# A new opening for a planned kernel of linear attention and a gated MLP: load order, fillers, first chunk, and the cost figures of the planner

## The chip, the core and the metric

The kernel runs on one core of one Trainium2 chip. A core has a matrix engine (PE, with its weight loads PEld), a vector engine (DVE), an activation engine (ACT), GpSimd (POOL) and SyncE (SP), which here only issues DMAs. The metric is the device time of one execution in microseconds (us). All inputs lie in HBM when the clock starts, the output has to be there when it stops.

## The reference, cut to what matters

For each of 4 x 8 heads a 48 x 48 state is read by q, corrected by k and v, token by token over 768 tokens; the result of all heads is the input of a gated MLP with 1536 hidden features.

```python
k_n = k / (norm(k) + 1e-6)
for t in range(S):
    y[:, :, t] = einsum('bhd,bhde->bhe', q[:, :, t], state)
    v_old = einsum('bhde,bhd->bhe', state, kt)
    state = state + bt * einsum('bhd,bhe->bhde', kt, vt - v_old)
x = y.transpose(0, 2, 1, 3).reshape(B * S, H * D)
out = (x @ w_a) * (x @ w_b) @ w_out
```

## The kernel before, in words

The 768 tokens are cut into 24 chunks of 32. Inside a chunk the recurrence is a triangular system, so a chunk needs: `prep` (norms of k, Gram matrices G of k and q on PE, scaled by `dc` on DVE), `solve` (a serial run of some 30 small DVE operations for four chunks at once, then transposes), and `steps`, a chain of small matmul groups per chunk with a copy by ACT or DVE between any two: W and X (they finish the solve of the first four chunks, behind an `eye` matmul), K (state times k, not for chunk 0), U (the corrected values), A (the output y), S (the state's update). Each group is 32 small matmuls, four of them side by side on four 32-row strips of PE, and since f32 goes through PE in two passes, it shows as 64 records. U, K and A write the two banks of the tile `duo`, S writes `S_ps`. Two chunks of y, transposed, are one tile `xb` of the MLP: per block of 128 hidden features (12 blocks) six matmuls `bank<-xb,wt`, a copy by ACT, a product by DVE, and two matmuls `bank<-wt,g` back. The first two pairs of chunks (24 MLP units) run in f32, the other ten in f16 halves after `split` has made these.

The weights come as 64-bit words, 1.15 MB a block, into three slots (`late` and two in `stage`); three DVE operations (`decode`) make f32 weights of a block in `wt` and free the slot. `scales` squares each block on ACT and sums the squares on PE (`bank<-one,sqw`).

Nothing is issued where it is written. Every call is noted as an `Op`, and `Plan.pack` lists them: a model of each engine's time, of the banks, of the DMAs (`MOVE`), of the matrix engine's clock and of its instruction blocks (`BLOCK`, `EDGE`, `FETCH`, `stall`) chooses for each engine which op comes next, by priorities that start from due times (`when`, `slot`). The planned order is then the program order of each engine. Until `UNTIL` one bank is kept aside, and where the model has PE at rest it puts fillers into that bank: matmuls `bank<-ones` of 128x512, whose result nobody reads (`issue`, line 484; all other instructions have line 493). `load` adds a DMA to SP's list; SP issues in order, and a load into a slot waits until the decode before it has read the slot. `hold` holds the number of the op that ends group A of chunk 1.

Of the kernel before, what the change touches and what calls it, by code (L numbers as in the profile page):

```python
# [26 lines left out]
P = 128  # L27
# [10 lines left out]
BASE, FRESH, UNIT = 46e3, 4.6e3, 3.75e3  # L38
# [11 lines left out]
def slot(c, piece):  # L50
    if c < 2:
        v = {
            0: {"W": -10, "X": -9, "U": -8, "S": -7, "A": -3.9},
            1: {"W": -6.9, "K": -6, "X": -5.9, "U": -5, "A": -4, "S": 0.2},
        }[c].get(piece, -30)
    elif c < 4:
        v = (c - 2) * 5 + {"W": 0.7, "X": 1.2, "K": 1.5, "U": 2.5, "S": 3.5, "A": 4.5}.get(piece, -30)
    elif piece == "G":
        v = 0.3 + 5 * (c // 2 - 2) if c < 8 else finish(c // 4 * 4 - 4 + c % 4 // 2) - 0.5
# [19 lines left out]
class Plan:  # L79
# [129 lines left out]
    def add(self, eng, fn, name, args, kw):  # L209
# [14 lines left out]
        if eng == "SP":  # L224
            op.dur = 475.0
            n = mybir.dt.size(outs[0].dtype)
            for d in outs[0].shape:
                n *= d
            op.move = max(n / 250.0, 20.0)
# [63 lines left out]

    def pack(self, pri, back=False):
# [10 lines left out]
        pos, edge, come, small = 0, self.EDGE, 0.0, False  # L305
        kept = 0 if back else 1
        vacant, held, blocked = [(k, {}) for k in range(len(self.pool) - kept)], {}, []
        fill = {}
# [3 lines left out]
        while len(done) < n:  # L312
# [56 lines left out]
            if not back and not o.banks and self.HOLD:  # L369

                soon = t + min(self.HOLD, 0.8 * o.dur)
                nxt_ = [r for r, k in wait[e] if t < r < soon and pri[k] < pri[i] - self.MARGIN]
                if nxt_:
                    heapq.heappush(can[e], (pri[i], i))
                    for x in can[e]:
                        heapq.heappush(wait[e], (min(nxt_), x[1]))
                    can[e] = []
                    continue
            at[i] = t
            if e == "PE" and not back:  # L380

                if kept:
                    f, took, many = max(free[e], self.SINCE), self.IDLE * (1 if warm else 2), 0
                    while f + took <= t:
# [3 lines left out]
                        took = self.IDLE * (1 if warm else 2)  # L388
                        use, f, many = use + took, f + took, many + 1
                    fill[i] = many  # L390
                    for _ in range(many):
                        pos += 4
                        if pos > edge:
                            edge, come = edge + self.BLOCK, t + self.FETCH
# [24 lines left out]
            if e == "SP":  # L419
                if back:  # L420
                    end = t + o.dur + self.MOVE[0] + o.move + self.MOVE[1]
                else:
                    dma = max(dma, t + o.dur + self.MOVE[0]) + o.move
                    end = dma + self.MOVE[1]
            done.append(i)
# [11 lines left out]
    HOLD = 300.0  # L437
# [4 lines left out]
    def order(self):  # L442
# [23 lines left out]
        for i, o in enumerate(ops):  # L466
            if o.banks and o.eng != "PE":
# [12 lines left out]
    def issue(self, tc):  # L480
        with tc.manual_schedule():
            for i in self.order():
                for _ in range(self.fill.get(i, 0)):
                    self.nc.tensor.matmul(  # L484
                        self.pool[-1][:, 0:512],
                        self.idle,
                        self.idle.unsqueeze(1).broadcast_to([P, 4, P]),
# [9 lines left out]
def tile_kernel(ctx, tc, kqt, kn, vn, beta, w, masks, picks, out):  # L497
# [88 lines left out]
    plan.idle = ones  # L586
    sqf = one("sqf", [P, 768])
# [29 lines left out]
    def decode(b):  # L617
        load(b, "w")
        st, d = slots[b % 3].rearrange("p (a l) -> p l a", l=2), wt[:, plain(b) : plain(b) + WD]
        lo, hi = st[:, 0], st[:, 1]  # L620
        V.tensor_scalar(d, hi, 5, 2, op0=ALU.logical_shift_left, op1=ALU.logical_shift_right)
# [3 lines left out]
        yield  # L625

# [96 lines left out]
    def load(c, what):  # L723
        if (c, what) in loaded:
            return
        loaded.add((c, what))
        if what == "w":
            SP.dma_start(slots[c % 3], w[c].bitcast(I32))
        elif what == "b":
            SP.dma_start(bt, beta)  # L730
            SP.dma_start(mk, masks)
        elif what == "m":
# [8 lines left out]
    def prep(g):  # L741
# [61 lines left out]
    def solve(g):  # L803
# [29 lines left out]
        V.transpose(XT.rearrange("p t u -> p (t u)"), X.rearrange("p t s -> p (t s)"))  # L833
        if HALVES[g]:

            xn = xnt.rearrange("p (a b) -> p a b", b=32)
            V.transpose(xn, X.rearrange("p t s -> p s t")[:, 0:16])
# [46 lines left out]
    def steps(g, chs):  # L884

        for c in chs:
            first, last = c == 0, c == NCH - 1
            rw, k2, vt = raw(c), knc(c), vnc(c)
            if HALVES[g]:
                join(g, c)  # L890
            if first:
                fs = [vt, vt]
            else:
                sh = shr()
                A.copy(sh, S_ps[0:KR, :, 0:384])
                plan.due = slot(c, "K")
                with plan.group():
# [14 lines left out]
            with plan.group():  # L912
                for q, h4, _, cols in heads():
                    T.matmul(
                        duo[tok(h4), h4 % 2, cols],
                        tts[c][tok(h4), q],
                        fs[h4 % 2][tok(h4), cols],
# [13 lines left out]
            with plan.group():  # L931
                for q, h4, a, cols in heads():
                    T.matmul(
                        duo[tok(h4 ^ 1), h4 % 2, cols],
                        ats[c][tok(h4), q],
                        u[tok(h4), h4 % 2, cols],
# [6 lines left out]
            if not last:  # L943
                plan.due = slot(c, "S")
                with plan.group():
                    for q, h4, a, cols in heads():
# [3 lines left out]
                            u[tok(h4), h4 % 2, cols],  # L950
# [6 lines left out]
            for h4 in range(4):  # L957
                A.copy(
                    y32[tok(h4 ^ 1)].rearrange("p (j b e) -> p b j e", j=3, b=4),
                    duo[tok(h4 ^ 1), h4 % 2, 0:384].rearrange("p (b j e) -> p b j e", b=4, j=3),  # L960
                )
            if c // 2 < FULL:
# [173 lines left out]
    for b in range(1, 3):  # L1136
        run_all(ws[b])
    run_all(st[0])
    queue.extend((s, list(range(NFC))) for s in range(2))
    load(0, "m")  # L1140
# [12 lines left out]
    def opening():  # L1153
        yield next(pr[1])
        for n in range(2):
            yield next(pr[1])
            yield next(pr[1])
            for _ in range(3):
                yield next(rest)
# [98 lines left out]
```

## Time and profile before

| | us |
|---|---|
| three runs | 636.98, 637.65, 635.96 (median 636.98) |
| profiled execution | 635.62, of which span 633.6 |
| PE busy | 614.3 |
| DVE busy | 411.1 |
| ACT busy | 305.0 |
| mean granted clock of PE | 0.978 |

The span runs from the first to the last instruction. Busy times are unions of an engine's instructions; PE also counts the fillers. The clock is given as a share of 2.4 GHz; PE runs at either 2.4 or 1.2 GHz (0.5).

### The profile page before, as it was taken

The numbers are of one execution on the slowest core, as the hardware profiler recorded it, in microseconds if no ns is written. First come the engines' busy times: TensorE is split into PE (matmuls) and PEld (weight loads), VectorE is DVE, ScalarE is ACT, GpSimd is POOL, SyncE is SP. The second block draws the span as 40 slices with busy tenths as digits, with TensorE's granted clock in tenths as the row PEclk, the third lists the DMA queues.
The fourth block names the chain that finished last, engine by engine and source line by source line (L and its number), as shares of the span: only waits on it lengthen the run. The fifth ranks groups of instructions, "written<-read, shape, count | busy, mean of one in ns | idle before, by whom it ended". The sixth has DMA issues, their size and how long they took to land.

```text
span 633.6 us, 25222 instructions
## 1 busy us (share of the span) xinstructions
PE 614.3 (97%) x11486; PEld 475.5 (75%) x11486; DVE 411.1 (65%) x1106; ACT 305.0 (48%) x750; POOL 23.8 (4%) x29
## 2 busy tenths in 40 slices
PE   8977989999999999999999999999999999999997
PEld 4445867777777878877878787887787787787785
DVE  4795597987779994389855589743788443244222
ACT  3043313458783475435654553654355455445322
POOL 0000030001000001100010000101000000000000
PEclk9966899999999999999999999999999999999999
DMA  9837456100200200301303103001000000000000
GB/s 278 286 137 254 172 178 206 40 25 3 85 27 28 85 27 28 110 2 37 103 3 111 28 3 110 27 4 53 2 4 27 3 27 3 3 26 2 26 1 26
DMA packets 10715, 41.19 MB, mean 65 GB/s; under 512 B 1200, under 2 KB 4656, under 8 KB 7728
## 3 DMA queue, kind: packets, MB, share of 16 engines
q1 hardware_dynamic: 10608, 39.57, 19.2%
q8 instruction: 90, 1.47, 1.0%
q14 instruction: 17, 0.14, 0.1%
HBM read 34.85 MB, written 4.72 MB: 62 GB/s over the span
## 4 chain that ended last, share of the span: by engine, by line
PE 86%; DVE 6%; ACT 6%; issue 2%; ACTq 0%
PE bank L493 67%; PE duo L493 13%; PE S_ps L493 3%; PE bank L484 3%; DVE b L493 2%; ACT wt L493 2%; ACT sqf L493 1%; DVE wt L493 1%; ACT y L493 1%; DVE tmp L493 1%; ACT sqy L493 0%; ACT a L493 0%; DVE at L493 0%; DVE g L493 0%; ACT tt L493 0%
## 5 line engine op out<-in xcount | busy, mean ns | idle before, releaser
L493 PE MATMUL bank<-xb,wt 128*128 128x256 f16 (+1 forms) x1800 | 247.8, 291 | 0.0
L493 PEld LDWEIGHTS <-wt 128*128 128x128 f16 x2160 | 208.3, 98 | 35.9 <-issue 1.0
L493 DVE TENSOR_TENSOR g<-bank,a 128x256 f32<-128x256 f32 x144 | 60.8, 423 | 128.3 <-ACT a L493 126.8
L493 PE MATMUL bank<-wt,ghl 128*128 128x384 f16 x720 | 136.5, 326 | 0.0
L493 ACT ACTIVATE a<-bank,gs 128x256 f32<-128x256 f32 x120 | 56.8, 474 | 147.7 <-PE bank L493 147.1
L493 PEld LDWEIGHTS <-ghl 128*128 128x128 f16 x720 | 67.2, 98 | 34.9
L493 PE MATMUL bank<-stage,wt 128*128 128x256 f16 x648 | 76.9, 273 | 0.0
L493 DVE TENSOR_TENSOR ghl<-g,ghl 128x256 f16<-128x256 f32 x120 | 52.0, 433 | 28.8 <-ACT ghl L493 27.9
L493 ACT CAST ghl<-g 128x256 f16<-128x256 f32 x120 | 48.3, 402 | 44.9 <-DVE g L493 44.3
L493 PEld LDWEIGHTS bank<-xb,wt 128*128 128x128 f32 x288 | 55.0, 194 | 12.8 <-issue 1.0
L493 DVE TENSOR_TENSOR b<-b,tmp 128x31 f32<-128x31 f32 (+20 forms) x170 | 56.6, 333 | 4.1
L493 DVE TENSOR_TENSOR tmp<-b,b 128x31 f32<-128x31 f32 (+20 forms) x170 | 56.3, 331 | 4.1
L493 ACT COPY y<-duo 32x384 f32<-32x384 f32 x96 | 45.1, 470 | 4.7 <-PE duo L493 3.6
L493 PE MATMUL bank<-wt,g 128*128 128x384 f32 x96 | 37.7, 511 | 0.0
L484 PE MATMUL bank<-ones 128*128 128x512 f32 x54 | 30.4, 713 | 3.0 <-DVE ones L493 3.0
L493 ACT COPY a<-bank 128x256 f32<-128x256 f32 x24 | 8.8, 369 | 41.6 <-PE bank L493 41.5
L493 PEld LDWEIGHTS duo<-sh,rawb 48*64 48x64 f32 x1216 | 20.2, 139 | 8.4 <-DVE at L493 3.5
L493 POOL TENSOR_TENSOR vnb<-vnb,nm 128x384 f32<-128x384 f32 x20 | 18.8, 963 | 176.5 <-DVE nm L493 83.2
L493 ACT COPY u<-duo 128x768 f32<-128x768 f32 (+1 forms) x27 | 20.2, 749 | 10.8 <-PE duo L493 7.0
L493 PE MATMUL duo<-sh,rawb 48*64 48x48 f32 x1216 | 22.6, 225 | 2.7 <-DVE at L493 1.8
L493 PEld LDWEIGHTS S_ps<-u,knb 32*48 32x48 f32 x1216 | 16.8, 126 | 10.9 <-issue 5.8
L493 DVE TENSOR_TENSOR f<-vnb,duo 128x768 f32<-128x768 f32 x23 | 21.8, 949 | 4.4 <-PE duo L493 4.0
(107 smaller groups left out, 586.5 us busy)
## 6 DMA issues: line engine op xcount, KB each, us to landing
stage<-in_w SPq DMA_DIRECT2D x8, 1152.0 KB, 7.2
rawb<-in_kqt SPq DMA_DIRECT2D x10, 896.0 KB, 5.9
vnb<-in_vn SPq DMA_DIRECT2D x12, 384.0 KB, 5.5
late<-in_w SPq DMA_DIRECT2D x4, 1152.0 KB, 6.5
out<-ob SPq DMA_DIRECT2D x24, 192.0 KB, 1.9
knb<-in_kn SPq DMA_DIRECT2D x10, 384.0 KB, 3.6
late<-in_kqt SPq DMA_DIRECT2D x2, 896.0 KB, 6.5
late<-in_kn SPq DMA_DIRECT2D x2, 384.0 KB, 4.3
```

What stands on the lines that cost most here:

```text
L484: self.nc.tensor.matmul(self.pool[-1][:, 0:512], self.idle, self.idle.unsqueeze(1).broadcast_to([P, 4, P]), start=True, stop=True, skip_gr ...
L493: fn(*(self.place(a, lease) for a in args), **{k: self.place(a, lease) for k, a in kw.items()})
```

## The change

The planner's figures change: `BASE` and `UNIT` of the due times are lower, loads over 1 MB are taken to be faster, an instruction block takes 2500 ns longer while DMAs run (`BUSY`), the waiting rule `HOLD` is replaced by one that holds until 40 us (`CALM`), and operations of ACT and DVE that read `duo` are given the priority of those that free a bank. Fillers may now be 128x128 (narrow) or 128x512, chosen by the length of the rest, and end at 42 us instead of 60; before everything else PE gets 47 small matmuls 32x48 on one 32x32 corner of the array (`PADS`).

Loads: beta comes second, the masks ahead of the first v, and four weight blocks belong to the early loads, the fourth straight into a part of `wt` that later blocks' results will fill (`place`; so do blocks 4 and 5). Every load that is not early waits for `hold`. `scales` is due 5.5 units later and waits for `hold` too.

First chunk: U, its copy, A and the copy of y use one bank of `duo` each, so one copy stands for four. The Gram matrices of chunks 2 and 3 go into banks of the pool instead of `duo`. Two of the four copies of y of chunk 1 go to DVE. After the first solve the transpose comes in two halves, the half that W reads first.

```diff
-BASE, FRESH, UNIT = 46e3, 4.6e3, 3.75e3
+BASE, FRESH, UNIT = 38e3, 4.6e3, 3.6e3
...
-EARLY = [(0, "k"), (2, "k"), (0, "r"), (2, "r"), (0, "b"), (0, "v"), (0, "w"), (2, "v"), (1, "w"), (2, "w")]
+EARLY = [(0, "k"), (0, "b"), (2, "k"), (0, "r"), (2, "r"), (0, "m"), (0, "v"), (0, "w"), (1, "w"), (2, "w"), (3, "w")]
 LAG = 2
+PADS = 47
...
-            edge, come = edge + self.BLOCK, enter + self.FETCH
+            edge, come = edge + self.BLOCK, enter + self.FETCH + (self.BUSY if enter < min(self.dma - self.MOVE[0], 110e3) else 0.0)
...
+                        wide = 4 if t - f > self.LONG else 1
...
-    BLOCK, EDGE, FETCH, AHEAD, STALL = 256, 193, 3500.0, 30, 250.0
-    IDLE, SINCE, UNTIL = 870.0, 1500.0, 60e3
+    BLOCK, EDGE, FETCH, BUSY, AHEAD, STALL = 256, 193, 3500.0, 2500.0, 30, 250.0
+    SINCE, UNTIL, LONG = 3500.0, 42e3, 900.0
...
+    plan.due = -1e6
+    with plan.group():
+        pad = att()
+        for _ in range(PADS):
+            T.matmul(pad[0:32, 0:48], ones[0:32, 0:32], ones[0:32, 0:48], start=True, stop=True, skip_group_check=True)
...
+    def place(b):
+        i = NFC - 1 - 2 * (b - 3)
+        return wt[:, i * WD : (i + 2) * WD] if 3 <= b < 6 else slots[b % 3]
...
-            plan.due = when(b + 2.5)
+            plan.due = when(b + 8)
+            plan.behind = set(hold)
             A.activation(sq, v, AF.Square)
...
         loaded.add((c, what))
+        plan.behind = set(hold)
         if what == "w":
-            SP.dma_start(slots[c % 3], w[c].bitcast(I32))
+            SP.dma_start(place(c), w[c].bitcast(I32))
...
-            ga = duo[:, ci % 2].rearrange("p (q n) -> p q n", n=64)
+            ga = (duo[:, ci % 2] if g or ci < 2 else att()).rearrange("p (q n) -> p q n", n=64)
...
+            for h in (1, 0):
+                r = slice(16 * h, 16 * h + 16)
+                V.transpose(XT[:, r].rearrange("p t u -> p (t u)"), X[:, r].rearrange("p t s -> p (t s)"))
...
+            side = lambda h4: 0 if first else h4 % 2
...
             if first:
-                for h4 in range(4):
-                    A.copy(u[tok(h4), h4 % 2], duo[tok(h4), h4 % 2, 0:384])
+                A.copy(u[:, 0], duo[:, 0, 0:384])
...
+                r, e = (slice(0, P), A.copy) if first else (tok(h4 ^ 1), V.tensor_copy if c == 1 and h4 < 2 else A.copy)
```

The order of PE's instructions at the program's start, up to the first group S, before. `rawb` is the raw k and q (groups G), `b_3_70` and `xn` the transposed solve (W, eye, X), `vnb` the first chunk's v (U), `u_72` its copy (S):

```order
L484 MATMUL bank_64<-ones 128x512 x7
L493 MATMUL duo<-rawb 32x64 x64
L484 MATMUL bank_64<-ones 128x512 x3
L493 MATMUL duo<-rawb 32x64 x64
L484 MATMUL bank_64<-ones 128x512 x13
L493 MATMUL bank_61<-b_3_70,tt_83 32x16 x32
L493 MATMUL bank_62<-b_3_70,mk 128x256
L493 MATMUL bank_63<-b_3_70,tt_84 32x16 x32
L493 MATMUL bank_62<-wr_91,xn 16x16 x32
L493 MATMUL bank_61<-b_3_70,mk 128x256
L493 MATMUL bank_61<-wr_92,xn 16x16 x32
L493 MATMUL duo<-vnb,tt_87 32x48 x32
```

And now:

```order
L498 MATMUL bank_61<-ones 32x48 x47
L489 MATMUL bank_64<-ones 128x512 x5
L489 MATMUL bank_64<-ones 128x128 x2
L498 MATMUL duo<-rawb 32x64 x64
L489 MATMUL bank_64<-ones 128x512 x2
L498 MATMUL bank_62<-rawb 32x64 x32
L498 MATMUL bank_63<-rawb 32x64 x32
L489 MATMUL bank_64<-ones 128x512 x13
L489 MATMUL bank_64<-ones 128x128 x2
L498 MATMUL bank_61<-b_3_70,tt_83 32x16 x32
L498 MATMUL bank_62<-b_3_70,tt_84 32x16 x32
L498 MATMUL bank_63<-b_3_70,mk 128x256
```

The first G now stands behind 47 small matmuls and 5 wide and 2 narrow fillers instead of 7 wide ones, and the third and fourth G have banks of their own. PE between U of chunk 0 and the first MLP matmul, now (`at_75`, `at_76` are A of chunks 0 and 1, `sh_73` is K, `f_71` is U):

```order
L498 MATMUL duo<-vnb,tt_87 32x48 x32
L489 MATMUL bank_64<-ones 128x128 x3
L498 MATMUL S_ps<-u_72,knb 48x48 x32
L498 MATMUL duo<-u_72,at_75 32x48 x32
L489 MATMUL bank_64<-ones 128x128 x3
L498 MATMUL duo<-sh_73,rawb 64x48 x32
L498 MATMUL duo<-f_71,tt_88 32x48 x32
L498 MATMUL duo<-u_72,at_76 32x48 x32
L498 MATMUL S_ps<-u_72,knb 48x48 x32
L498 MATMUL bank_62<-b_3_70,tt_85 32x16 x32
L498 MATMUL bank_63<-xb,wt 128x256 x6
```

Before, four sums of squares `bank<-one,sqw`, four wide fillers, and eye and X of chunk 2 stood among these rows; all of them have left this place. SP's list, before and then now:

```order
L493 DMA knb<-in_kn 128x768 x2
L493 DMA rawb<-in_kqt 112x2048 x2
L493 DMA bt<-in_beta 128x192
L493 DMA mk<-in_masks 128x160
L493 DMA vnb<-in_vn 128x768
L493 DMA late<-in_w 128x2304
L493 DMA vnb<-in_vn 128x768
L493 DMA stage<-in_w 128x2304 x2
```

```order
L498 DMA knb<-in_kn 128x768
L498 DMA bt<-in_beta 128x192
L498 DMA knb<-in_kn 128x768
L498 DMA rawb<-in_kqt 112x2048 x2
L498 DMA mk<-in_masks 128x160
L498 DMA vnb<-in_vn 128x768
L498 DMA late<-in_w 128x2304
L498 DMA stage<-in_w 128x2304 x2
L498 DMA wt<-in_w 128x2304
L498 DMA vnb<-in_vn 128x768
L498 DMA wt<-in_w 128x2304
```

The last row here, block 4, is the first that waits for group A of chunk 1. On DVE the first instruction is now the memset of `ones`, which the fillers read; before it was the fourth.

## Rows read from the trace of the kernel before

**Rows 1.** The page: busy time, share of the span and instructions of each engine; the DMA queue that brings PE's and the other engines' instructions (packets, MB, share).

```profile
PE 614.3 (97%) x11486; PEld 475.5 (75%) x11486; DVE 411.1 (65%) x1106; ACT 305.0 (48%) x750; POOL 23.8 (4%) x29
...
q8 instruction: 90, 1.47, 1.0%
```

**Rows 2.** Busy time by stretch of the span (us): length, then busy time and instructions of PE, PEld, DVE, ACT and POOL, granted clock, DMA share, GB/s.

```profile
31.50:33.80 2.30, 0.00 (x0) 0.01 (x1) 2.16 (x6) 0.00 (x0) 0.00 (x0) 1.00 0.01 5
...
33.80:64.83 31.03, 25.40 (x870) 17.35 (x870) 22.62 (x26) 14.13 (x30) 0.95 (x1) 0.65 0.61 213
64.83:67.20 2.37, 2.37 (x14) 1.92 (x7) 2.30 (x3) 0.85 (x2) 0.00 (x0) 0.50 0.85 315
...
94.50:97.90 3.40, 3.34 (x80) 2.55 (x80) 3.33 (x4) 2.06 (x4) 0.00 (x0) 0.50 0.89 337
...
193.48:600.00 406.52, 406.52 (x7922) 324.56 (x7918) 258.21 (x772) 209.32 (x534) 12.79 (x15) 1.00 0.11 34
...
64.83:193.48 128.65, 124.68 (x2169) 96.97 (x2161) 102.00 (x234) 65.86 (x156) 9.85 (x9) 0.98 0.27 88
```

**Rows 3.** The timeline of the opening up to group W of chunk 0: start, duration, engine, line, operation, out<-in, count, idle time before and what ended it.

```profile
3.02 9.32 PE L484 MATMUL bank<-ones 128*128 128x512 f32 x14 [3.02 <-DVE ones L493]
...
12.26 1.99 PE L493 MATMUL duo<-rawb 48*32 48x64 f32 x128
...
14.17 0.19 DVE L493 TENSOR_TENSOR dc<-s,bt 128x32 f32<-128x32 f32 x1 [4.08 <-DMA bt<-in_beta]
...
18.60 1.53 PE L493 MATMUL duo<-rawb 48*32 48x64 f32 x64 [0.55 <-DVE at L493]
...
21.86 0.60 DVE L493 TENSOR_TENSOR b<-duo,dc 128x256 f32<-128x256 f32 x1 [0.44 <-ACT tt L493]
...
22.49 1.25 DVE L493 STREAM_TRANSPOSE b<-b 128x1024 f32<-128x1024 f32 x1
...
32.44 1.25 DVE L493 STREAM_TRANSPOSE b<-b 128x1024 f32<-128x1024 f32 x1
...
33.83 0.73 PE L493 MATMUL bank<-b,tt 32*32 32x16 f32 x64 [2.34 <-DVE b L493]
```

**Rows 4.** PE's weight loads of the first fillers in the timeline; a wide filler has two, one for each pass over its 512 columns.

```profile
8.30 0.34 PEld L484 LDWEIGHTS bank<-ones 128*128 128x128 f32 x1 [0.52 <-issue]
9.15 0.20 PEld L484 LDWEIGHTS bank<-ones 128*128 128x128 f32 x1 [0.52 <-issue]
9.60 0.19 PEld L484 LDWEIGHTS bank<-ones 128*128 128x128 f32 x1 [0.24 <-issue]
```

**Rows 5.** DMA issues and the time from issue to landing (last number): the raw k and q of chunks 0 and 1, and beta; then, from the timeline, SP's issue of the raw k and q of chunks 0 to 3.

```profile
rawb<-in_kqt SPq DMA_DIRECT2D x1, 896.0 KB, 8.9
...
bt<-in_beta SPq DMA_DIRECT2D x1, 96.0 KB, 11.5
...
1.64 0.89 SPq L493 DMA_DIRECT2D rawb<-in_kqt  x2
```

**Rows 6.** PE's timeline between group X of chunk 0 and the first MLP matmul.

```profile
36.13 0.57 PE L493 MATMUL bank<-wr,xn 32*16 32x16 f32 x46
37.66 0.36 PE L493 MATMUL bank<-wr,xn 32*16 32x16 f32 x18 [0.96 <-issue]
37.95 1.22 PE L493 MATMUL bank<-b,mk 128*128 128x256 f32 x2
39.10 0.74 PE L493 MATMUL bank<-wr,xn 32*16 32x16 f32 x64
39.70 1.13 PE L493 MATMUL duo<-vnb,tt 32*32 32x48 f32 x43
41.50 0.69 PE L493 MATMUL duo<-vnb,tt 32*32 32x48 f32 x21 [0.67 <-issue]
...
47.82 0.53 PE L493 MATMUL duo<-u,at 32*32 32x48 f32 x29 [1.07 <-issue]
...
54.43 1.50 PE L493 MATMUL duo<-f,tt 32*32 32x48 f32 x64
...
60.76 1.20 PE L493 MATMUL S_ps<-u,knb 32*48 32x48 f32 x47 [2.09 <-issue]
...
64.83 0.79 PE L493 MATMUL bank<-xb,wt 128*128 128x256 f32 x1
```

**Rows 7.** ACT's and DVE's timeline in the same stretch: the copies of U and y of chunk 0, and a decode.

```profile
42.24 1.95 ACT L493 COPY u<-duo 32x384 f32<-32x384 f32 x4 [0.66 <-PE duo L493]
...
48.40 1.92 ACT L493 COPY y<-duo 32x384 f32<-32x384 f32 x4 [1.72 <-PE duo L493]
...
55.93 0.75 DVE L493 TENSOR_SCALAR wt<-stage 128x1152 int32<-128x1152 int32 x1
...
56.72 2.77 DVE L493 SCALAR_TENSOR_TENSOR wt<-stage,wt 128x1152 int32<-128x1152 int32 x2
```

**Rows 8.** PE's timeline in the MLP's f32 units: groups U, W and S of later chunks, and the two longest rests of PE after 67 us.

```profile
89.29 0.88 PE L493 MATMUL duo<-f,tt 32*32 32x48 f32 x64
...
90.94 0.74 PE L493 MATMUL bank<-b,tt 32*32 32x16 f32 x64
...
94.56 0.56 PE L493 MATMUL S_ps<-u,knb 32*48 32x48 f32 x14 [2.12 <-issue]
...
164.87 1.15 PE L493 MATMUL duo<-sh,rawb 48*64 48x48 f32 x64 [1.34 <-DVE at L493]
```

More of the change, by code (lines that the diff above doesn't have):

```diff
@@ L228, in add @@
                 n *= d
-            op.move = max(n / 250.0, 20.0)
+            op.move = max(n / (350.0 if n > 1e6 else 240.0), 20.0)
         else:
@@ L305, in pack @@
         pos, edge, come, small = 0, self.EDGE, 0.0, False
+        self.dma = 0.0
         kept = 0 if back else 1
         vacant, held, blocked = [(k, {}) for k in range(len(self.pool) - kept)], {}, []
-        fill = {}
+        fill, idle = {}, Op("PE")
         for i, o in enumerate(ops):
@@ L368, in pack @@
             o = ops[i]
-            if not back and not o.banks and self.HOLD:
-                soon = t + min(self.HOLD, 0.8 * o.dur)
+            if t < self.CALM and not o.banks:
+                soon = t + o.dur
                 nxt_ = [r for r, k in wait[e] if t < r < soon and pri[k] < pri[i] - self.MARGIN]
@@ L382, in pack @@
                 if kept:
-                    f, took, many = max(free[e], self.SINCE), self.IDLE * (1 if warm else 2), 0
-                    while f + took <= t:
+                    f, many = max(free[e], self.SINCE), []
+                    while True:
                         while until <= f:
@@ L387, in pack @@
                             use, until = 0.0, until + self.WINDOW
-                        took = self.IDLE * (1 if warm else 2)
-                        use, f, many = use + took, f + took, many + 1
+                        wide = 4 if t - f > self.LONG else 1
+                        idle.words, idle.dur = 4, (213.0 * wide + 10.0) * (1 if warm else 2)
+                        step = self.stall(idle, f, pos, edge, come)
+                        if f + step[0] + idle.dur > t:
+                            break
+                        many.append(wide)
+                        use, f = use + idle.dur, f + step[0] + idle.dur
+                        pos, edge, come = step[1:]
                     fill[i] = many
[L391 to L394, printed above, removed]
                 while until <= t:
@@ L466, in order @@
         for i, o in enumerate(ops):
-            if o.banks and o.eng != "PE":
+            if (o.banks or "duo" in str([k[0] for k in o.rd])) and o.eng != "PE" and o.stream != "prep0":
                 pri[i] = min([pri[i]] + [pri[k] + self.SOON for k in o.deps if ops[k].eng == "PE"])
@@ L482, in issue @@
             for i in self.order():
-                for _ in range(self.fill.get(i, 0)):
+                for n in self.fill.get(i, []):
                     self.nc.tensor.matmul(
-                        self.pool[-1][:, 0:512],
+                        self.pool[-1][:, 0 : n * P],
                         self.idle,
-                        self.idle.unsqueeze(1).broadcast_to([P, 4, P]),
+                        self.idle.unsqueeze(1).broadcast_to([P, n, P]),
                         start=True,
@@ L726, in load @@
         loaded.add((c, what))
+        plan.behind = set(hold)
         if what == "w":
-            SP.dma_start(slots[c % 3], w[c].bitcast(I32))
+            SP.dma_start(place(c), w[c].bitcast(I32))
         elif what == "b":
             SP.dma_start(bt, beta)
+        elif what == "m":
             SP.dma_start(mk, masks)
-        elif what == "m":
+        elif what == "s":
             SP.dma_start(sel, picks)
@@ L891, in steps @@
             if first:
[L892 removed]
+                fs = [vt]
             else:
@@ L896, in steps @@
                 plan.due = slot(c, "K")
+                plan.behind = set(opened[:1] if c == 2 else ())
                 with plan.group():
@@ L933, in steps @@
                     T.matmul(
-                        duo[tok(h4 ^ 1), h4 % 2, cols],
+                        duo[tok(h4 ^ 1), 1 if first else side(h4), cols],
                         ats[c][tok(h4), q],
-                        u[tok(h4), h4 % 2, cols],
+                        u[tok(h4), side(h4), cols],
                         start=(first and q == 0),
@@ L957, in steps @@
             for h4 in range(4):
-                A.copy(
-                    y32[tok(h4 ^ 1)].rearrange("p (j b e) -> p b j e", j=3, b=4),
-                    duo[tok(h4 ^ 1), h4 % 2, 0:384].rearrange("p (b j e) -> p b j e", b=4, j=3),
-                )
+                r, e = (slice(0, P), A.copy) if first else (tok(h4 ^ 1), V.tensor_copy if c == 1 and h4 < 2 else A.copy)
+                e(
+                    y32[r].rearrange("p (j b e) -> p b j e", j=3, b=4),
+                    duo[r, 1 if first else h4 % 2, 0:384].rearrange("p (b j e) -> p b j e", b=4, j=3),
+                )
+                if first:
+                    break
             if c // 2 < FULL:
@@ L1135, in tile_kernel @@
     run_all(sv[0])
-    for b in range(1, 3):
-        run_all(ws[b])
+    run_all(ws[1])
     run_all(st[0])
+    run_all(ws[2])
     queue.extend((s, list(range(NFC))) for s in range(2))
-    load(0, "m")
+    load(0, "s")
     V.tensor_copy(sum16, sel[:, 0:P])
@@ L1155, in opening @@
         for n in range(2):
+            for _ in range(3):
+                yield next(rest)
             yield next(pr[1])
             yield next(pr[1])
-            for _ in range(3):
-                yield next(rest)
         yield from chain([rest, pr[1]])
```

21 lines of the change are left out of this document (12 added, 9 removed).

## The prediction

> **What bounds the kernel now.** The page first: PE is busy in 97% of the span, no other engine in more than 75% [rows 1]. That is an average. By stretch, PE has no rest at all from 193.48 to 600 us [rows 2], so a cause that makes the first 193 us shorter moves all that follows forward, one for one. Up to 64.83 PE is mostly filled with work nobody reads, and waits. So the question is when the MLP's first matmul can start (64.83 now, [rows 6]), what useful work has been done by then, and what rests come behind it. Read the opening in three pieces: to the transpose of the first Gram matrices (22.49), the serial solve on DVE (to 32.44), and the chain of small groups from W of chunk 0 (33.83) to 64.83 [rows 3, 6].
>
> In the first piece DVE waits 4.08 us for beta, which lands 11.5 us after its issue behind 2.5 MB of others [rows 3, 5]. In the third, PE's clock is at 0.65 on the mean, and PE rests four times with nobody to blame but "issue" [rows 2, 6]. Between the rests at 37.66 and 41.50 lie 18 + 2 + 64 + 43 = 127 matmul records, each with its weight load: 254 instructions. The queue that brings instructions moves 1.47 MB in 90 packets, 16 KB each [rows 1]. I read these rests as the wait for the next block of some 256 instructions, and the distance from one release to the next as the time that such a block takes: 3.84 us from 37.66 to 41.50, while the DMA queues were nearly idle, and 6.32 from 41.50 to 47.82, while weights were loading [rows 6]. A group of 32 small matmuls is half a block, so the chain can't run faster than two groups in a block time.
>
> The Trainium skill, "Runtime: NRT & Kernel Launch", section "Instruction fetch mechanics", has the same blocks of 256, but says that the fetch is mostly hidden, as instructions are dispatched more slowly than they arrive. Small matmuls here go out faster, and the rows show rests of 0.67 to 2.12 us; by the page's rule they would be something else, and the third piece would be bound by its engines alone: first MLP matmul at 47.8 + 1.2 = 49.0 below, and a sum 5.0 us shorter, 626.9.
>
> **The change part by part, first piece.** `ones` is written first, so PE starts at 1.2 instead of 3.02 (DVE starts at 1.02, a memset of 0.17 us). Then 47 small matmuls, 94 records, on one corner of the array. No row has these alone. A group U has 64 records on four strips, 16 a strip, in 1.50 us at half clock and 0.88 at full clock [rows 6, 8]. If the corner shared like four strips, 94 records cost 2.2 us at half clock; if each waits for the one before, 94/16 x 1.50 = 8.8 us. One corner is one strip, so I take the latter. Before, fillers went from 0.85 us a pass to 0.45 at 9.15, 6.1 us after PE's first matmul at 3.02 [rows 3, 4]. With the rise 6.1 us after the start as well, 65 records run slowly until 7.3, the other 29 take 29/16 x 0.88 = 1.6: 8.9. Five wide fillers are ten passes of 0.43, two narrow ones together one pass: G starts at 13.6. It can't start before its data, 1.64 + 8.9 us plus beta's 0.3 [rows 5], so the ends are 10.9 and 1.2 + 8.8 + 11 passes at 0.85 = 19.4.
>
> From 13.6: G of chunks 0 and 1 1.99, two wide fillers 1.7, G of chunks 2 and 3 1.99 and a rest of about 0.55 as now [rows 3]: 19.8. The copy 0.37, the product 0.60 and a mask product 0.40 follow: transposes start at 21.2, against 22.49. The first two products no longer wait for beta, nor G for `duo`; that gain of over 4 us is mostly eaten by G's later start. The solve keeps its 9.95 us; W needs only the first half of the transpose that took 1.25, so 0.6 more. W starts at 33.83 - 1.3 - 0.6 = 31.9.
>
> **Third piece.** From W of chunk 0 to the first MLP matmul there are now twelve groups, so six blocks. By the order, W of chunk 1 holds the first release point, at 32.9. Engine pace first, with the durations of these rows: two W 1.4, two eye with X 2.2, U and its input copy 1.3, one copy of u 0.5 in place of four in 1.95 [rows 7], S 0.9, the copy of the state 0.8 (A and the one copy of y, 0.5 for four in 1.92, lie beside it), K 1.15, f 0.95, U 0.9, u 0.8, A 0.9, two copies of y on each of two engines 1.0, the transpose 0.6: 13.4, and ten handoffs of 0.25: 47.8. Block pace: 32.9 + 5 x 3.84 + 0.7 for the rest of W of chunk 2 = 52.8 with idle queues; 32.9 + 5 x 6.32 + 0.7 = 65.2 with loads in flight. Early loads are 8.1 MB by the shapes in SP's list; before, all of 8.7 MB had landed by 33 us, where the DMA share falls to 0.01 [rows 2]. Later loads wait for chunk 1. So I take idle queues, and add 1.2 for groups at half clock that are longer than the rest they fill: 54.0, that is 10.8 earlier. Ends: 47.8 and 65.2.
>
> The first chunk's U and A now write one bank from four strips. The W group does the same today, and its 64 records take 0.74 [rows 8], which shows no turn-taking, so I charge nothing. The Trainium skill, "TensorEngine Tiling (Array Packing)", section "Gotcha 1: PSUM Pressure", says that row tiles can't access one bank at the same time. By it U and A, now two strips to a bank, would double: 2 x 0.88 = 1.8 us, and the sum would be 633.7. W's 0.74 speaks against it.
>
> **Behind the first MLP matmul.** Eye and X of chunk 2 (0.6 + 0.74) and four sums of squares at 0.15 now fall behind it: +1.9. They were hidden in the opening. The half clock from 64.83 to 67.20 costs 1.2 now [rows 2]; a start out of small groups will be at half clock again, so I leave it. New due times reorder units after 193 us, where PE never rests [rows 2]; nothing is charged for that. The held loads: behind the first held one, block 4, stand all others in SP's list, so eight blocks and the chunks from 4 on all load beside the MLP. And DVE: three operations of 0.75 + 2.77 us make a block [rows 7]; five were decoded before 64.83, now two and a third before the first MLP matmul. That puts 2.7 x 3.5 = 9.4 us on a DVE that is busy 102.0 of 128.65 us up to 193.48 [rows 2]: some 87%. Loads beside small groups make block rests. The row of today is 2.12 us at 94.56 with a half clock after it until 97.90, 3.40/2 = 1.7 lost: 3.8 together [rows 2, 8]; a second rest of 1.34 at 164.87 follows two G groups, a whole block [rows 8]. Bounds: all of these gone, -5.2; three more full ones, +11.4. I take one more, +3.8.
>
> **Sum.** -10.8 + 1.9 + 3.8 = -5.1 us on the execution's own 635.62: 630.5. That execution was 1.4 below the median of the runs, so the median becomes 631.9.
>
> **Rivals.** (1) Slower: the rests move instead of going. With loads and decodes in the MLP's f32 units, each state group that meets a block boundary while loads fly costs 3.8. The start's gain is 8.9 net; with one extra I have 631.9, with three 639.5, with four 643.3. Slower than 0.3% begins at three extra. For it: eight block loads and 2.7 decodes move there; against: the planner now adds block time while DMAs run, and a rest needs two small groups within a block. (2) No change: fillers overshoot. If PE stays at half clock through all the pads and fillers, G starts at 19.4, 5.8 late, and the sum is 637.7; two extra rests give 635.7. Against the first: the clock rose in 6.1 us at the present start. (3) Much faster: no block rest behind the first MLP matmul at all, neither extra nor old: -8.9 - 5.2, 622.9; with the chain at engine pace too, 6.2 less, 616.7. Against it: eight block loads fly there. (4) The changes do not act: loads held too short, so that blocks take 6.32: first MLP matmul at 65.2, 0.4 + 1.9 + 3.8 on top, 643.1; SP's list speaks against it.
>
> **How the numbers follow.** A measurement of this kernel can tell 0.3%, 1.9 us. Forecast (one extra rest, give or take one, 626 to 635): 0.52. Faster than that (3): 0.15. Rival 2, 635.1 to 638.9: 0.16. Rivals 1 and 4, above 638.9: 0.17. So faster 0.67, same 0.16, slower 0.17. The likeliest case's own range is 626 to 635. The range for 8 in 10 leaves out half of each outer case: 623.5 to 640.5.
>
> **What would show it.** Right: beta no longer named as a wait of `dc`; G's first record at 13 to 14 us with the pads taking 7 us or more; transposes near 21; W near 32; the first `bank<-xb,wt` at 52 to 56; four releases about 3.8 us apart in the chain; rests of PE behind it, of 1 to 3 us, at S, A or K groups, and a half clock after one of them. Wrong: pads done in 2 us (G at 11); a first MLP matmul after 58; PE waiting for DVE's decode (`wt`) or for weight loads in the f32 units; stretches of half clock after 100 us longer than now; or PE at rest anywhere in 200 to 600 us.

## The result and the profile after

| | us |
|---|---|
| before, six runs | 635.76 to 637.65, median 636.56 |
| after, six runs | 639.86 to 643.75, median 640.59 |
| ratio, 95% interval | 1.0074, 1.0049 to 1.0098 |
| profiled execution after | 640.76, of which span 638.7 |

The change made the kernel slower by 0.7%. The forecast was 631.9, with 623.5 to 640.5 as its range.

First PE's timeline of the opening after the change, with the columns of [rows 3]:

```profile
1.05 7.72 PE L498 MATMUL bank<-ones 32*32 32x48 f32 x94 [1.05 <-DVE ones L498]
8.70 7.84 PE L489 MATMUL bank<-ones 128*128 128x512 f32 x14
16.47 1.99 PE L498 MATMUL duo<-rawb 48*32 48x64 f32 x128
...
24.05 0.44 PE L498 MATMUL bank<-rawb 48*32 48x64 f32 x17 [1.99 <-issue]
24.42 13.57 PE L489 MATMUL bank<-ones 128*128 128x512 f32 x30
37.91 1.30 PE L498 MATMUL bank<-b,tt 32*32 32x16 f32 x128
...
42.46 0.88 PE L498 MATMUL duo<-vnb,tt 32*32 32x48 f32 x64
...
45.91 0.92 PE L498 MATMUL S_ps<-u,knb 32*48 32x48 f32 x59 [1.48 <-issue]
...
49.91 0.38 PE L489 MATMUL bank<-ones 128*128 128x128 f32 x1 [1.52 <-issue]
...
60.03 1.35 PE L498 MATMUL bank<-xb,wt 128*128 128x256 f32 x5 [1.01 <-DVE xb L498]
```

The first G starts 4.2 us later than in [rows 3] (16.47 against 12.26), W of chunk 0 4.1 later (37.91 against 33.83). The chain from W to the first MLP matmul takes 22.1 us instead of 31.0, and so that matmul comes 4.8 us earlier than in [rows 6]. Yet the span ends 5.1 us later: behind this point 9.9 us have been added (578.7 us from 60.03 to 638.7, against 568.8 from 64.83 to 633.6). Busy time by stretch, columns as in [rows 2] for PE alone:

```profile
60.03:100.00 39.97, 37.17 (x752) 1.00 0.68 240
100.00:193.48 93.48, 89.45 (x1512) 1.00 0.17 52
193.48:300.00 106.52, 104.93 (x2194) 1.00 0.15 46
300.00:400.00 100.00, 99.30 (x2104) 1.00 0.21 62
400.00:500.00 100.00, 97.25 (x1914) 1.00 0.05 15
500.00:600.00 100.00, 100.00 (x1662) 1.00 0.03 10
600.00:638.70 38.70, 35.09 (x281) 1.00 0.06 21
```

Length less busy time is rest. From 193.48 to 500 us, where PE had none [rows 2], it now rests 1.6 + 0.7 + 2.75 = 5.0 us. Up to 193.48 it rests 2.8 + 4.0 = 6.8 us behind the first MLP matmul, against 4.0 before (128.65 less 124.68, [rows 2]). The last 2.05 us of the 9.9 are PE's busy time behind this point, which grew by as much (563.2 us against 561.15). In it are the groups that moved there (24 records of `bank<-one,sqw`, 2 of `bank<-b,mk` and 56 of `bank<-wr,xn` more than before), but not they alone: the half clock that followed this point before, 0.50 in two stretches of 2.37 and 3.40 us [rows 2], is gone, for the granted clock (the third figure from the right) reads 1.00 in every row. So other work must have grown too; which, is left open here. The groups of instructions from 193.48 to 500 us name the place of the late rests (busy time, mean ns of one, idle time before it and what ended it):

```profile
L498 PE MATMUL bank<-n,sum 128*128 128x4 bf16 x14 | 2.3, 166 | 4.2 <-DVE n L498 2.8 <-DVE g L498 1.3
```

This is the small matmul that adds up the norm of y. It needs four squares on ACT (`sqy`) and a cast on DVE (`n`). At one of its two longest rests, ACT, DVE and PE show:

```profile
403.59 0.29 ACT L498 ACTIVATE sqy<-y 128x96 f32<-128x96 f32 x1
403.77 0.20 ACT L498 ACTIVATION_READ_ACCUMULATOR sqy<-y 128x1 f32 x1
403.86 0.84 ACT L498 ACTIVATE sqf<-knb 128x768 f32<-128x768 f32 x1
404.60 0.28 ACT L498 ACTIVATE sqy<-y 128x96 f32<-128x96 f32 x1
...
404.73 0.95 DVE L498 TENSOR_REDUCE ss<-sqf 128x16 f32<-128x768 f32 x1 [0.58 <-ACT sqf L498]
405.60 0.16 DVE L498 CAST n<-n 128x4 bf16<-128x4 f32 x1
...
406.14 0.16 PE L498 MATMUL bank<-n,sum 128*128 128x4 bf16 x1 [1.06 <-DVE g L498]
```

`sqf` (0.84 us) squares the k of a later chunk, and nobody waits for it yet. It stands between the third and the fourth `sqy`, and its sum `ss` (0.95 us) stands on DVE ahead of the cast. PE waits for both. The releaser in brackets, `g`, is only what DVE finished last; the line above shows the cast at 405.60.

Last, SP's issues after the first ones:

```profile
14.38 0.33 SPq L498 DMA_DIRECT2D wt<-in_w  x1
14.76 0.43 SPq L498 DMA_DIRECT2D knb<-in_kn  x1
15.31 0.35 SPq L498 DMA_DIRECT2D wt<-in_w  x1
18.10 0.33 SPq L498 DMA_DIRECT2D rawb<-in_kqt  x1
58.20 0.33 SPq L498 DMA_DIRECT2D knb<-in_kn  x1
```

The first four are loads that "wait for `hold`", block 4 first among them. A of chunk 1 runs at 55; they go out at 14 to 18, and the last of them lands 21.2 us after its issue, at 39.3. `plan.behind` is a dependence of the plan alone: it gives the load its place in SP's list, but the DMA writes a place that nobody uses, so nothing of chunk 1 holds the instruction. (SP's waits up to here end, in the trace, with landings of earlier loads.) Only the load at 58.20 is held, by the buffer that it overwrites: SP waits 39.7 us for group S, which reads it.

### The profile page after: what moved, and what is told of

Read it like the earlier page. It is cut to its first block, busy times and chain, and to the rows that moved or that the text cites. A ratio compares the mean times of both kernels' runs of the same rounds, so it can differ in the third digit from the quotient of the medians.

```text
span 638.7 us, 25412 instructions
## 1 busy us (share of the span) xinstructions
PE 614.2 (96%) x11586; PEld 479.2 (75%) x11586; DVE 406.4 (64%) x1109; ACT 299.7 (47%) x742; POOL 24.2 (4%) x29
## 4 chain that ended last, share of the span: by engine, by line
PE 65%; DVE 23%; ACT 8%; issue 3%; ACTq 0%
PE bank L498 50%; PE duo L498 10%; DVE b L498 8%; DVE tmp L498 5%; PE bank L489 4%; PE S_ps L498 2%; ACT y L498 2%; DVE g L498 2%; DVE ghl L498 2%; DVE f L498 1%; ACT tt L498 1%; DVE wt L498 1%; ACT sqf L498 1%; ACT wt L498 1%; DVE at L498 1%
## 5 line engine op out<-in xcount | busy, mean ns | idle before, releaser
L498 PEld LDWEIGHTS bank<-xb,wt 128*128 128x128 f32 x288 | 53.5, 190 | 12.3 <-DVE xb L498 1.1
L498 ACT COPY y<-duo 32x384 f32<-32x384 f32 (+1 forms) x91 | 42.7, 469 | 5.8 <-PE duo L498 4.1
L489 PE MATMUL bank<-ones 128*128 128x512 f32 (+1 forms) x60 | 25.5, 580 | 1.5 <-issue 1.5
L498 PEld LDWEIGHTS duo<-f,tt 32*32 32x32 f32 x1472 | 18.0, 107 | 11.1 <-issue 6.9
L498 ACT COPY u<-duo 128x768 f32<-128x768 f32 (+1 forms) x24 | 18.8, 784 | 15.4 <-PE duo L498 15.4
L498 PE MATMUL duo<-u,at 32*32 32x48 f32 x1536 | 22.3, 206 | 3.6 <-issue 2.7
L498 PE MATMUL duo<-f,tt 32*32 32x48 f32 x1472 | 21.4, 206 | 3.9 <-issue 2.8
```

Of the source, the lines that this page charges most:

```text
L489: self.nc.tensor.matmul(self.pool[-1][:, 0 : n * P], self.idle, self.idle.unsqueeze(1).broadcast_to([P, n, P]), start=True, stop=True, ski ...
L498: fn(*(self.place(a, lease) for a in args), **{k: self.place(a, lease) for k, a in kw.items()})
```

## The experiments

Three suspects follow: the 94 serial records of the pads, loads that fly where the plan has none, and an edit to which the prediction gave no price, `HOLD` replaced by `CALM`. Under the old rule an operation of ACT or DVE without a bank stood back if a more urgent one was to be ready within 0.3 us; the new one ends at 40 us of the plan. What the new one does before 40 us, where it looks ahead over the whole length of an operation, no run tests by itself.

**Run 1, pads over four strips.** The order of all instructions stays as it is.

```diff
-        for _ in range(PADS):
-            T.matmul(pad[0:32, 0:48], ones[0:32, 0:32], ones[0:32, 0:48], start=True, stop=True, skip_group_check=True)
+        for h in range(PADS):
+            r = slice(32 * (h % 4), 32 * (h % 4) + 32)
+            T.matmul(pad[r, 0:48], ones[r, 0:32], ones[r, 0:48], start=True, stop=True, skip_group_check=True)
```

> The changed kernel with one edit: the 47 opening matmuls go in turn to four strips of the array instead of all to one corner. Theory A (the opening lost its time to 94 records one after another at half clock): the pads take about 2.2 us (1.05 to 3.3) instead of 7.65, the clock rises near 9 us instead of 14.45, group G starts at 10.7 to 12 (its k and q land at 10.6) instead of 16.47, W of chunk 0 at 30 to 33 instead of 37.91, the first MLP matmul 5 to 8 us before 60.03, and the whole kernel takes 632.5 to 636. Rival B (the chain behind W is paced by loads and instruction blocks that do not start sooner): G and W move as above, but the chain takes 25 us or more in place of 22.1, the first MLP matmul stays at 58 or later, and the kernel takes 638.5 to 641.

Measured: 639.36 (636.39 to 644.69), ratio to before 1.0051, 1.0026 to 1.0076. Its PE timeline:

```profile
1.05 2.14 PE L498 MATMUL bank<-ones 32*32 32x48 f32 x94 [1.05 <-DVE ones L498]
3.12 5.96 PE L489 MATMUL bank<-ones 128*128 128x512 f32 x14
11.37 3.19 PE L498 MATMUL duo<-rawb 48*32 48x64 f32 x128 [2.28 <-DMA rawb<-in_kqt]
...
31.80 1.29 PE L498 MATMUL bank<-b,tt 32*32 32x16 f32 x128 [0.23 <-DVE b L498]
...
38.80 0.63 PE L498 MATMUL bank<-wr,xn 32*16 32x16 f32 x52 [2.75 <-issue]
...
56.19 5.87 PE L498 MATMUL bank<-xb,wt 128*128 128x256 f32 x18 [0.97 <-DVE xb L498]
```

Theory A has the first piece right: pads 2.14 us, G bound by its data, W 6.1 us sooner. Of these 6.1 only 3.8 reach the first MLP matmul, since the chain now takes 24.4 us and rests 2.75 us inside group X. So rival B is right in its mechanism and in the kernel's time (638.5 to 641), though its chain of 25 us and its first MLP matmul at 58 did not come. Whether any of it reaches the end can't be told from the medians: the interval overlaps that of the change.

**Run 2, the look-ahead back.**

```diff
-            if t < self.CALM and not o.banks:
-                soon = t + o.dur
+            if (t < self.CALM or not back) and not o.banks:
+                soon = t + (o.dur if t < self.CALM else min(300.0, 0.8 * o.dur))
```

> The changed kernel with one edit: after the first 40 us of the plan an operation without a bank again stands back, as in the kernel before, when a more urgent one of its engine is to be ready within 0.3 us. Theory C (the rests of PE at the norm's sums behind 193 us come from long operations that start on ACT and DVE just ahead of the norm's short ones): PE rests less than 1 us from 193.5 to 500 in place of 5.0, and the kernel takes 635.5 to 637.5 with the first MLP matmul unchanged near 60. Rival D (these rests come from the new due times or the new rule for readers of the shared banks): rests of 4 to 5 us remain there, and the kernel takes 640 to 641.5.

Measured: 634.73 (630.42 to 638.6), ratio 0.9965, 0.994 to 0.9991. PE by stretch:

```profile
193.48:300.00 106.52, 105.91 (x2197) 1.00 0.16 46
300.00:400.00 100.00, 100.00 (x2109) 1.00 0.21 61
400.00:500.00 100.00, 99.86 (x1993) 1.00 0.05 15
```

The rests fall from 5.0 to 0.75 us, and the kernel is 5.9 us faster than the change. Theory C holds, but 634.73 is 0.8 below its range, and the rests are worth only 4.3 of the 5.9. The first MLP matmul comes at 58.35 in this run's trace, though the edit leaves the opening as it was; run 4, with the same opening, has it at 58.89. So up to 1.7 us of this matmul's place differ from execution to execution. The same work around the same sum, ACT and then PE:

```profile
399.91 0.28 ACT L498 ACTIVATE sqy<-y 128x96 f32<-128x96 f32 x1
...
401.13 0.84 ACT L498 ACTIVATE sqf<-knb 128x768 f32<-128x768 f32 x1
...
401.00 0.17 PE L498 MATMUL bank<-n,sum 128*128 128x4 bf16 x1
```

`sqf` now comes behind the last `sqy`, and PE has no idle time in front of the sum.

**Run 3, both edits.**

> Both edits of the two runs beside it. If theories A and C hold, their gains add, since the one lies before 40 us and the other behind 193 us: 628 to 632. If only A holds 632.5 to 636, if only C 635.5 to 637.5, if neither 639 to 641.5.

Measured: 632.19 (629.83 to 634.29), ratio 0.9937, 0.992 to 0.9954. That is 0.2 above the range for both, and under either edit alone (634.73 and 639.36). Against the change, the look-ahead alone gave 5.9 us; the medians give the strips another 2.5 on top of it, but the intervals of runs 2 and 3 overlap. Inside group X of chunk 1 PE rests as in run 1:

```profile
39.85 0.64 PE L498 MATMUL bank<-wr,xn 32*16 32x16 f32 x52 [2.76 <-issue]
```

**Run 4, the old rule of urgency.**

```diff
-            if (o.banks or "duo" in str([k[0] for k in o.rd])) and o.eng != "PE" and o.stream != "prep0":
+            if o.banks and o.eng != "PE":
```

> The changed kernel with the old rule of urgency: only ACT's and DVE's operations that use a pooled bank inherit PE's urgency, not the readers of the two shared banks. PE's order stays as it is. Theory C: the rests at the norm's sums stay, 4 to 5 us from 193.5 to 500, and the kernel takes 639.5 to 642. Rival D1 (the rule is their cause): they fall below 1.5 us, and the kernel takes 635.5 to 637.5.

Measured: 641.95, ratio 1.0092, 1.0076 to 1.0108; rests of 1.4 + 0.6 + 2.5 us in the same stretches. The rule is not the cause of the rests.

**Run 5, the converse: the kernel before, its look-ahead ended at 40 us.**

```diff
-            if not back and not o.banks and self.HOLD:
+            if not back and not o.banks and self.HOLD and t < 40e3:
```

> The kernel before with one edit: the look-ahead of the planner (an operation without a bank stands back when a more urgent one of its engine is to be ready within 0.3 us) ends at 40 us of the plan. Theory C (losing the look-ahead is what cost the changed kernel its rests behind 193 us): PE, which had no rest from 193.5 to 600, now rests 3 to 6 us there, most of it ahead of the norm's sums, and the kernel takes 639.5 to 643 instead of 636.7. Rival D (the rests came from the due times or another edit of the change): less than 1 us of rest, 636 to 638.

Measured: 641.46, ratio 1.0075, 1.0059 to 1.0091. This one edit makes the kernel before as slow as the whole change. Its PE by stretch:

```profile
193.48:300.00 106.52, 105.31 (x2191) 1.00 0.16 46
300.00:400.00 100.00, 99.37 (x2119) 1.00 0.21 62
400.00:500.00 100.00, 97.09 (x1915) 1.00 0.05 15
```

1.2 + 0.6 + 2.9 = 4.7 us of rest where there was none, and 4.7 us more time. Theory C holds from this side too.

**Run 6, the loads really held.** To run 3 one copy of one element is added. It makes a true write-after-write: the load of block 4 must wait for DVE, and all behind it in SP's list with it.

```diff
                 A.copy(u, duo[:, :, 0:384])
+            if c == 1:
+                V.tensor_copy(place(4)[0:1, 0:1].bitcast(F32), u[0:1, 0, 0:1])
             yield
```

> Run 3 (four strips, look-ahead back) and one copy of one element: DVE writes it into block 4's place once u of chunk 1 is there, so that the load of block 4, and with it all behind it in SP's list, waits on the chip for chunk 1, as the plan takes it to. The instructions stand as in run 3 otherwise. Theory E (the four loads that fly until 41 us slow the instruction blocks of the chain): the rest of 2.76 us inside group X of chunk 1 falls below 1, the first MLP matmul comes at 53.5 to 55 instead of 56.31, and the kernel takes 629 to 631 instead of 632.2. Rival F (3.6 MB more to load beside the MLP's first units costs more than that): rests of PE from 60 to 110 us grow by 2 us or more, and the kernel takes 632.5 to 637.

Measured: 629.76 (628.55 to 631.84), ratio 0.9893, 0.9874 to 0.9912. SP's list and PE's chain:

```profile
48.75 0.33 SPq L498 DMA_DIRECT2D wt<-in_w  x1
```

```profile
32.52 1.29 PE L498 MATMUL bank<-b,tt 32*32 32x16 f32 x128 [0.38 <-DVE b L498]
...
36.47 0.92 PE L498 MATMUL bank<-wr,xn 32*16 32x16 f32 x64
...
43.99 0.38 PE L489 MATMUL bank<-ones 128*128 128x128 f32 x1 [1.02 <-issue]
...
50.90 0.24 PE L498 MATMUL S_ps<-u,knb 32*48 32x48 f32 x1 [0.56 <-issue]
...
52.36 4.15 PE L498 MATMUL bank<-xb,wt 128*128 128x256 f32 x18 [0.55 <-DVE xb L498]
```

X of chunk 1 (the second line) is now one run of 64 records without a rest; in run 3, with the same instructions, PE rested 2.76 us inside it, and in run 1, 2.75. The chain takes 19.8 us instead of 23.5; its mean granted clock is 0.91 instead of 0.75. Theory E holds; the first MLP matmul comes 1.1 us sooner still than its range. By their traces the two runs have the same order on PE, ACT and DVE but for the one copy, at 48.58, behind these rests; up to there they differ in when four loads fly. The other runs agree. With strips and the loads in flight PE rests in X in run 7 (5.49 us) and run 8 (4.13) as well; with strips and held loads it has no rest there in runs 9 and 11.

Beside the MLP PE then rests 2.05 us before 65.62, 1.74 before 73.15 and 2.03 before 104.35. Run 3 has the first and the last of these at the same groups (2.12 and 0.91). Its rests from 60 to 110 us, 3.0 us, grow to 5.8, as rival F had it, but that is less than the chain gains.

The Trainium skill, "Runtime: NRT & Kernel Launch", section "Instruction fetch mechanics", has the fetch of instructions mostly hidden. PE's rest marked "issue" comes and goes here with the loads in flight; read as the wait for the next block, as the prediction reads it, the fetch is not hidden in groups of small matmuls.

**Run 7, the plan told the truth instead.** To run 3: loads have no `plan.behind`.

```diff
         loaded.add((c, what))
-        plan.behind = set(hold)
```

> Run 3 with the other remedy: the plan no longer holds the loads behind chunk 1, so it knows that they fly early and prices the instruction blocks for it; SP's list and the order of the units change. Theory E: what flies early stays early, the rests of the chain are filled or planned around, 629 to 632. Rival F2 (the order then puts still more loads into the chain): the first MLP matmul comes after 57, and the kernel takes 632.5 to 637.

Measured: 636.42, ratio 0.9998, 0.9984 to 1.0013. Rival F2: PE rests 5.49 us in X and 3.02 in S, and the first MLP matmul comes at 63.02. Pricing the loads does not help when more of them fly in the chain.

**Run 8, the old due times.** To run 3:

```diff
-BASE, FRESH, UNIT = 38e3, 4.6e3, 3.6e3
+BASE, FRESH, UNIT = 46e3, 4.6e3, 3.75e3
```

> Run 3 with the due times of the kernel before (46 and 3.75 us in place of 38 and 3.6). If these figures cost nothing behind 193 us, as the prediction has it: 631 to 633.5, and no rest over 1 us from 193.5 to 600. If they matter (theory D2): below 630.5 or above 634.

Measured: 631.72, ratio 0.9935, 0.9912 to 0.9958; 0.8 us of rest from 193.5 to 500. The due times cost nothing, as the prediction had it.

**Runs 9 to 11, parts of run 6.** Run 9 loads the first k and q sooner, run 10 has no pads, run 11 has U and A of the first chunk in two banks.

```diff
-EARLY = [(0, "k"), (0, "b"), (2, "k"), (0, "r"), (2, "r"), (0, "m"), (0, "v"), (0, "w"), (1, "w"), (2, "w"), (3, "w")]
+EARLY = [(0, "k"), (0, "b"), (0, "r"), (2, "k"), (2, "r"), (0, "m"), (0, "v"), (0, "w"), (1, "w"), (2, "w"), (3, "w")]
```

```diff
-PADS = 47
+PADS = 0
```

```diff
-            side = lambda h4: 0 if first else h4 % 2
+            side = lambda h4: h4 % 2
...
-                A.copy(u[:, 0], duo[:, 0, 0:384])
+                for h4 in range(4):
+                    A.copy(u[tok(h4), h4 % 2], duo[tok(h4), h4 % 2, 0:384])
```

> Run 6 (strips, look-ahead, loads really held) with the k and q of chunks 0 and 1 loaded ahead of the second block of norm data. In run 6 the first G starts at 12.26, when they land. Theory G (their landing sets the start): they land near 8.8, the first G starts before 10.5, the second G, which still needs the k and q of chunks 2 and 3 at 15.8, before 17.2 instead of 17.72; W of chunk 0 comes 0.5 to 1.5 us sooner and the kernel takes 628 to 629.5. Rival H (the norms, whose data now come later, delay the products by as much): W not sooner, 629.5 to 631.

Measured: 632.71 (629.07 to 634.89), ratio 0.9919, 0.9893 to 0.9945. G starts at 10.27, yet W at 32.37, 0.15 sooner than in run 6: PE waits there for the solve on DVE. Rival H's mechanism: `dc`, made from the norms, comes at 17.16 instead of 12.21. The kernel's time is no gain, and above the ranges of both.

> Run 6 without the 47 small matmuls. Theory I (they do nothing but pass time before the first k and q land): G starts within 0.5 us of 12.26, W of chunk 0 within 1 us of 32.52, and the kernel takes 628.5 to 631.5. Rival J (their 94 records place the limits of the instruction blocks): G and W as said, but the chain from W to the first MLP matmul takes over 22 us in place of 19.8, and the kernel takes 632 to 635.

Measured: 631.02, ratio 0.9902, 0.9879 to 0.9925; G at 11.91, W at 32.83, a chain of 20.6 us. The pads do nothing that can be measured here (theory I); the intervals of runs 6 and 10 overlap.

> Run 6 with U and A of the first chunk in two banks again, four copies of u and four of y, as in the kernel before. If the chain runs at the pace of the instruction blocks (the prediction's step), the longer copies lie beside the wait for the next block: the chain takes 19.5 to 20.8 us, 629 to 631. If it runs at the pace of its engines, four copies of u in 1.95 us instead of one in 0.5 cost 1.4 or more: the chain takes 21.2 to 23, 631 to 633.5.

Measured: 631.27, ratio 0.9917, 0.989 to 0.9944. The chain takes 20.55 us, in the range for the pace of instruction blocks; the time, 631.27, lies at the lower end of the other range (631 to 633.5), and the rests from 193.48 to 300 are 2.2 us instead of run 6's 0.6. The planner also put wide fillers in place of narrow ones beside the longer copies. So this run does not decide it.

**Run 12, held loads with the pads on one corner.** Run 6 with run 1's edit undone.

> Run 6 with the 47 small matmuls back on one corner, that is the changed kernel with the look-ahead back and the loads really held. In run 2, the same without the held loads, W of chunk 0 stood near 37.4 and the loads were down at about 39, so almost none flew in the chain. Theory K (held loads and strips need each other: the hold pays only where the chain starts while loads fly): within 1.2 us of run 2's 634.7, that is 633.5 to 636. Rival L (the two are worth the same apart as together): 2.4 us under run 2, 631.5 to 633.

Measured: 635.7 (632.25 to 637.5), ratio 0.9981, 0.9966 to 0.9997: theory K. W comes at 37.13, and the chain takes 20.9 us with the held loads against 21.0 in run 2 without. With slow pads the chain starts when the early loads have landed, so there is nothing to hold. The other way round, run 6 and this run differ in the pads alone, and their intervals lie apart: with held loads and the look-ahead the strips are worth 5.9 us (629.76 against 635.7).

## Why the prediction was wrong

The sum was 630.5 for the profiled execution; it took 640.76, 10.2 us more. Of these 6.0 lie in the opening (first MLP matmul 4.8 earlier instead of 10.8) and 4.2 behind it (9.9 added instead of 5.7). This is one execution; runs 2 and 4 show 1.7 us of difference in the opening alone.

**Point by point.**

- *"New due times reorder units after 193 us, where PE never rests; nothing is charged for that."* This step failed, by 5.0 us, and it is the largest single miss. The due times are innocent (run 8), the urgency of the readers of `duo` too (run 4). It was the lost look-ahead, which the change names and the prediction gave no price (runs 2 and 5). That PE has no rest in a stretch of before says that the order there was good. It doesn't say that any order would be.
- *The pads: "With the rise 6.1 us after the start as well".* That they run one after another was right. That they took 7.65 us where 7.7 was worked out is luck: the 7.7 has the clock rise inside the pads, at 7.3, and without that rise the same sum gives 8.8. The fillers behind them still took 0.85 us a pass up to some 14.4, about 5.7 us after the first wide one. So G started at 16.47 instead of 13.6; the rest in G of chunk 3 was 1.99 us instead of 0.55. The transposes came at 25.72, 4.5 late. That is the mechanism of the prediction's second rival, priced there at 637.7, though the clock did rise before the last fillers.
- *W at 31.9.* Besides these 4.5, the wide fillers under the solve ran until W's start at 37.91, with a stretch at half clock (0.50 from 24.69 to 28.10), and W waited for them; the transpose that it needs is in the two halves that DVE began at 35.65 (1.31 us for both). The list of fillers had been taken as free.
- *The chain, 22.1 us.* Measured 22.1, but by luck. The reason given, "later loads wait for chunk 1", was false: they flew until 39, and the chain found quiet queues only because it began at 38. Run 1 shows the chain with them, 24.4 us, run 6 without, 19.8. Nor is it shown that the pace of instruction blocks sets the chain. Of the "four releases about 3.8 us apart" two came, at 45.91 and 49.91, 128 records apart. The chain's rests are 3.0 us marked "issue" and 3.0 for results of DVE and ACT; in run 6 they are 1.6 and 2.6. So both count.
- *One more block rest behind it, +3.8.* That was a rest of 2.1 and a half clock worth 1.7. Rests up to 193.48 grew by 2.9 us; no half clock came with them, and the one behind the first MLP matmul, which the sum left as it was, went too.
- *Moved work, +1.9.* Busy time grew by 2.05, but that is not the moved work alone. By the prediction's own prices the half clock that is gone gave back 1.2 + 1.7 = 2.9, so other work grew by about 3 us (an estimate from these prices). That the figures agree is luck.
- *One bank for U and A of chunk 0, nothing charged.* Right: U took 0.88 us for 64 records, as the U of later chunks [rows 8]. The doubling that the Trainium skill's "TensorEngine Tiling (Array Packing)", section "Gotcha 1: PSUM Pressure", would make of it (1.8 us) did not show.

Run 6 comes nearest to what the prediction took the change for: loads held, no rest by a worse order, and pads that do not delay G (they lie on four strips, though, not on a corner). There W comes at 32.52 (31.9 was forecast), the first MLP matmul at 52.36 (54.0), 6.9 us are added behind it (5.7), and the median is 629.76 (631.9). The terms miss by up to 2.3 us there, and in part cancel. What failed for the change itself is that the program's words on its loads, its order and its pads were taken for what the chip would do.

## What to carry to other kernels

A dependence in a planner is not a wait on the chip: for each "held" load ask which buffer, read or written by whom, makes the instruction wait, and look at its issue in the trace. A planner's rule that decides who goes first touches every stage, so an edit of one needs a price even where the engine never rests; look for long operations without urgency that now stand ahead of short ones with it. And a head start for a chain pays in full only if what the chain needs is free at the new time: here loads in flight at the earlier start gave PE 2.75 us of rest in run 1.

## What was not expected of the hardware

94 records on one 32x32 corner keep PE busy for 7.65 us, and still they did not bring the clock up: in the four kernels with the pads there (the change, runs 2, 4 and 12) the wide fillers that start at 8.70 still take 0.85 us a pass in the pass that begins at 12.28, and the first quick one begins between 13.66 and 14.65. PE's weight loads, one for each pass of a filler, show the step from 0.85 us a pass to 0.43. The column of the granted clock reads 1.00 all the while, but 0.85 us is what a pass takes from 24.69 to 28.10, where that column reads 0.50 (1.2 GHz). The change:

```profile
13.98 0.34 PEld L489 LDWEIGHTS bank<-ones 128*128 128x128 f32 x1 [0.52 <-issue]
14.65 0.19 PEld L489 LDWEIGHTS bank<-ones 128*128 128x128 f32 x1 [0.33 <-issue]
```

With the pads over four strips, the wide fillers start at 3.12, and the step comes at about 5 in run 1:

```profile
4.13 0.34 PEld L489 LDWEIGHTS bank<-ones 128*128 128x128 f32 x1 [0.52 <-issue]
4.99 0.24 PEld L489 LDWEIGHTS bank<-ones 128*128 128x128 f32 x1 [0.52 <-issue]
5.47 0.19 PEld L489 LDWEIGHTS bank<-ones 128*128 128x128 f32 x1 [0.24 <-issue]
```

Over the seven runs with strips the first quick pass begins between 4.99 and 7.36, so run 1 is the earliest. Without pads and with fillers from 3.02 it begins at 6.52 in run 10 and at 9.15 before the change [rows 4]. So the corner is told apart by its time, 12 us and more after PE's start at 1.05; that the strips bring the clock up sooner than no pads at all is not shown, and what distinguishes the corner is not settled beyond these times.
